# One PSUM ring of four double banks and a new hand-written order, in an attention and maxout-FFN kernel

## The chip, the cores and the metric

The kernel runs on 1 core of one Trainium2 chip. The metric is the device time in microseconds; the time before is the median of 8 runs.

## The reference

Attention over memory slots, then a feed-forward block with a maximum of three products. Batch 8, 8 heads, sequence 576, head size 64, 32 slots, model width 512, d_ff 768; all in float32.

```python
a = np.exp(phi - max_s(phi));  a = a / (sum_s(a) + 1e-09)      # over the sequence
k_m = einsum('bhsm,bhsd->bhmd', a, k);  v_m = einsum('bhsm,bhsd->bhmd', a, v)
attn = softmax_m(q @ k_m.T / 8)                                # over the 32 slots
o = attn @ v_m                                                 # heads side by side: 512 columns
h = max(max(o @ w1, o @ w2), o @ w3)
out = h @ w_out                                                # 4608 x 512
```

## The kernel before

The kernel never forms `o`. As `o @ w` is `attn @ (v_m @ w)`, it folds each batch's 32 slots per head into the weights (8 heads x 32 slots = 256 rows) and multiplies `attn` by the folded weights. It also uses max(x1, x2, x3) = max(x1 - x3, x2 - x3, 0) + x3: w1 - w3 and w2 - w3 are folded, the rectified first difference is compared with the second one, and x3 @ w_out is added through w3 @ w_out, which is worked out once at the start.

Work is cut into steps that are named by a letter, a number and the batch (`F3@2`). Each function issues the instructions of one step, and a text written by hand gives the order of all steps; each engine runs its own instructions in that order. The text lists the steps of the first batches one by one, then a loop runs the same pattern for the middle batches (a `+` after a name is a later batch, a `-` an earlier one), and a last line does batch 7. The steps:

- L0, L1, L2 (lines 92, 99, 107): loads of phi, of k and v, and of q; from batch 1 on all are issued by GpSimd's queue, which also loads the weights at the start and takes its work in order. Each load waits until the buffer of two batches earlier is free.
- E (line 208, ScalarE): exp of phi. B (line 219): 72 small matmuls into `kvp`, the sums over the sequence. N (lines 233 to 243, VectorE): division. K (lines 259, 261): three transposes into `kvtp`, copied by VectorE to `kvt`.
- Q0, Q1 (line 271, VectorE): transposes of q, one per half of the heads. S (lines 293, 302): 32 small matmuls into two `sc` accumulators, and two exps on ScalarE.
- M (line 314): two matmuls for the sums over slots. R (lines 327, 333, ScalarE): logarithm, then exp, for the reciprocal. X (line 338, VectorE): the product, which is `attn`.
- D0 to D3 (line 358): the folds, 8 matmuls each; D0 to D2 make the 1536 columns of `wp` (D0: columns 0 to 511, and so on), D3 makes `wp3`. Each takes a drain of 128 x 1024 out of PSUM (`evacuate`, lines 148 to 158).
- F0 to F11 (lines 383 to 395): first layer, 4 matmuls each into `acc`. An even F is the first difference of a column tile and ends in a relu on ScalarE (`h1`, four buffers), the odd one after it in number ends in a maximum on VectorE that reads `h1`.
- T0 to T4 (lines 411 to 429): second layer, 128 rows of output each, 6 matmuls with w_out and 2 with `wp3` (4 small ones in T4, which spans two batches and comes with odd batches); drained by `evacuate` and stored by SyncE's queue (line 442).
- W, O, V (lines 167, 175, 191): w3 transposed, w3 @ w_out, and the differences of the weights, all only at the start. Z (line 143): dummy matmuls on a tile of zeros.

Accumulators come from two rings of PSUM tiles. `acc_pool` holds three tiles of two banks each, for B, S (two tiles), M, D and F; `one_pool` holds two tiles of one bank, for K, W, O, T and Z. A tile of a ring is taken in the order of the text, and the first matmul into it waits until the tile that was there before has been read.

`EVAC` says who drains: "a" is ScalarE, "v" VectorE, and "s" shares it, half each. The last T is drained by both engines, half each, and stored by two queues.

Of the kernel before, what the change touches and what calls it, by code (L numbers as in the profile page):

```python
# [8 lines left out]
FP32 = mybir.dt.float32  # L9
BF16 = mybir.dt.bfloat16  # L10
# [5 lines left out]
def kernel(  # L16
# [12 lines left out]
    nc = tc.nc  # L29

    B, H, S, D = q.shape
    M = phi.shape[-1]
    P = 128
    NP = H // 2
    NG = NP // 2
# [3 lines left out]
    DM = H * D  # L39
    DF = moe_w1.shape[1]  # L40
    FT = DF // P
# [6 lines left out]
    quad = ctx.enter_context(tc.tile_pool(name="quad", bufs=4))  # L48
    opool = ctx.enter_context(tc.tile_pool(name="opool", bufs=6))
    acc_pool = ctx.enter_context(  # L50
        tc.tile_pool(name="accp", bufs=3, space=bass.MemoryType.PSUM)
    )
    one_pool = ctx.enter_context(
        tc.tile_pool(name="onep", bufs=2, space=bass.MemoryType.PSUM)
    )

    ctx.enter_context(tc.manual_schedule())
# [13 lines left out]
    wo_sb = const.tile([P, FT, DM], BF16, name="wo_sb")  # L71
# [10 lines left out]
    halves = [slice(0, NP // 2), slice(NP // 2, NP)]  # L82
# [55 lines left out]

    def warm_up(n):

        po = one_pool.tile([P, DM], FP32, name="po", tag="one")
        for _ in range(n):
            nc.tensor.matmul(  # L143
                po[:, 0:BANK], lhsT=warm[:, 0:P], rhs=warm, start=True, stop=True
            )


    EVAC = {"D": "asaa", "T": "vaava"}

    def evacuate(kind, n, out_, in_):  # L150
        e = EVAC[kind][n]
        if e == "s":
            nc.scalar.copy(out=out_[:, 0], in_=in_[:, 0])  # L153
            nc.vector.tensor_copy(out=out_[:, 1], in_=in_[:, 1])  # L154
        elif e == "a":
            nc.scalar.copy(out=out_, in_=in_)  # L156
        else:
            nc.vector.tensor_copy(out=out_, in_=in_)  # L158


    def w3_t(f2):

        pt = one_pool.tile([P, 2, NP, P], BF16, name="pt", tag="one")
        for i in range(2):
            f = 2 * f2 + i
            for j in range(NP):
                nc.tensor.transpose(
                    pt[:, i, j, :], w_sb[:, j, 2, f * P : (f + 1) * P], ident
                )
        nc.vector.tensor_copy(out=w3T[:, 2 * f2 : 2 * f2 + 2], in_=pt)  # L170

    def w3_o(j):
        po = one_pool.tile([P, DM], FP32, name="po", tag="one")
        for f in range(FT):
            nc.tensor.matmul(  # L175
                po,
                lhsT=w3T[:, f, j, :],
                rhs=wo_sb[:, f, :],
                start=(f == 0),
                stop=(f == FT - 1),  # L180
            )
        nc.scalar.copy(out=w3o[:, j, :], in_=po)
# [27 lines left out]
    def att_kv(b, js=range(NP)):  # L210
        s = st[b]
        if "kvp" not in s:
            s["kvp"] = acc_pool.tile([P, NG, BANK], FP32, name="kvp", tag="acc")
        kv, kvp = loaded[b]["kv"], s["kvp"]
        for c in range(NC):
            for j in js:
                for a in range(NG):
                    r = slice(HP * a, HP * (a + 1))
                    nc.tensor.matmul(  # L219
                        kvp[M * j : M * (j + 1), a, 0 : 3 * D],  # L220
                        lhsT=s["e"][r, j, c, :],
                        rhs=kv[r, :, j, c, :],
                        start=(c == 0),
                        stop=(c == NC - 1),
                        tile_position=(HP * a, M * j),
                    )
# [26 lines left out]
    def att_kv_t(b):  # L253


        s = st[b]
        ps = one_pool.tile([P, 3, P], BF16, name="kvtp", tag="one")
        for n in range(3):
            nc.tensor.transpose(ps[:, n], s["kvn"][:, n], ident)
        kvt = work.tile([P, 3, P], BF16, name="kvt")  # L260
        nc.vector.tensor_copy(out=kvt, in_=ps)
        s["kvt"] = kvt
# [13 lines left out]
    attns = {}  # L276
# [68 lines left out]
    wps, wp3s = {}, {}  # L345
# [25 lines left out]
    hts = {}  # L371
# [32 lines left out]
    def ffn2(b, t, last=False):  # L404


        hT, attn = hts[b // 2], attns[b // 2]
        po = one_pool.tile([P, DM], FP32, name="po", tag="one")
        c0 = S - HP if t == 4 else (b % 2) * (S + HP) + t * P
        for fc in range(FT):  # L410
            nc.tensor.matmul(  # L411
                po,
                lhsT=hT[:, fc, c0 : c0 + P],
                rhs=wo_sb[:, fc, :],
                start=(fc == 0),
                stop=False,
            )
        for g in range(NG):
            if t < 4:
                nc.tensor.matmul(  # L420
                    po,
                    lhsT=attn[:, g, c0 : c0 + P],
                    rhs=wp3s[b][:, g, :],
                    start=False,
                    stop=(g == NG - 1),
                )
            else:
                for u in range(2):
                    nc.tensor.matmul(  # L429
                        po[HP * u : HP * (u + 1)],  # L430
                        lhsT=attn[:, g, c0 + HP * u : c0 + HP * (u + 1)],
                        rhs=wp3s[b - 1 + u][:, g, :],
                        start=False,
                        stop=(g == NG - 1),
                        tile_position=(0, HP * u),
                    )
        ot = opool.tile([P, DM], FP32, name="ot")
        r0 = (b // 2) * 2 * S + c0
        rows = out[r0 : r0 + P, :]
        if not last:  # L440
            evacuate("T", t, ot, po)
            nc.sync.dma_start(out=rows, in_=ot)
        else:
            h = [slice(0, DM // 2), slice(DM // 2, DM)]
            nc.scalar.copy(out=ot[:, h[0]], in_=po[:, h[0]])
            nc.vector.tensor_copy(out=ot[:, h[1]], in_=po[:, h[1]])
            nc.scalar.dma_start(out=rows[:, h[0]], in_=ot[:, h[0]])
            nc.sync.dma_start(out=rows[:, h[1]], in_=ot[:, h[1]])


    def issue(b, n):

        if not 0 <= b < B or (n == "T4" and b % 2 == 0):
            return
        i = int(n[1:]) if len(n) > 1 else None
        {
            "L": lambda: (load_ph, load_kv, load_q)[i](b),
            "E": lambda: [att_exp(b, h) for h in (halves if b == 0 else [slice(0, NP)])],
            "B": lambda: [att_kv(b, range(NP)[h]) for h in (halves if b == 0 else [slice(0, NP)])],
            "N": lambda: att_kv_norm(b),  # L460
            "K": lambda: att_kv_t(b),
            "Q": lambda: att_q(b, i),
            "S": lambda: att_score(b),
            "M": lambda: att_sum(b, i),
            "R": lambda: att_rec(b, i),
            "X": lambda: att_mul(b, i),
            "D": lambda: fold(b, i),
            "F": lambda: ffn1(b, i),
            "T": lambda: ffn2(b, i),
            "W": lambda: w3_t(i),  # L470
            "O": lambda: w3_o(i),
            "V": lambda: w_diff(i),
            "Z": lambda: warm_up(i),
        }[n[0]]()

    def run(b, text):

        for w in text.split():
            issue(b + w.count("+") - w.count("-"), w.rstrip("+-"))

    for w in """
        E@0 L0@2 Z26@0 B@0 N@0 Z5@0 K@0 Q0@0 Q1@0 L2@2 L1@2 Z18@0 W1@0 W0@0 S@0 M0@0 R0@0
        W2@0 M1@0 O1@0 O0@0 V0@0 R1@0 O3@0 X0@0 X1@0 D0@0 V2@0 O2@0 F6@0 F2@0 F4@0 V1@0 F0@0
        D2@0 D1@0 F7@0 F3@0 E@1 L0@3 F8@0 F1@0 F9@0 F5@0 F10@0 F11@0 B@1 L1@3 D3@0 N@1 K@1
        D0@1 Q1@1 Q0@1 L2@3 D2@1 D1@1 T2@0 S@1 T0@0 E@2 L0@4 M0@1 R0@1 M1@1 X0@1 R1@1 X1@1
        T3@0 T1@0 Q1@2 F0@1 F8@1 F1@1 F9@1 F6@1 F2@1 D3@1 B@2 L1@4 Q0@2 L2@4 F4@1 N@2 F7@1
        K@2 F10@1 F3@1 S@2 F5@1 F11@1 M1@2 E@3 L0@5 M0@2 R1@2 R0@2 T0@1 D0@2 X0@2 D2@2 B@3
        L1@5 N@3 X1@2 T1@1 D1@2 D3@2 Q0@3 Q1@3 L2@5 K@3 E@4 L0@6
    """.split():
        n, b = w.split("@")  # L490
        issue(int(b), n)
    for b in range(2, B - 1):
        run(b, "F6 F0 T4- F7 F4 F1 F2 F10 F3 F8 F5 F9 T2- S+ Q0++ B++ L1++++ D3+ E+++")
        run(b, "L0+++++ N++ T3- M0+ R0+ M1+ F11 X0+ T0 R1+ X1+ Q1++ L2++++ D0+ D2+ D1+")
        run(b, "T1 K++")
    run(B - 1, "T4- F0 F2 F1 F10 F8 F11 F3 T3- F4 F6 F5 F7 F9 T2- T2 T3 T4 T0")
    ffn2(B - 1, 1, last=True)


# [28 lines left out]
```

The softmax here doesn't subtract the row's maximum and nothing guards it: scores larger than these inputs give would overflow.

## Time and profile before

| | us |
|---|---|
| median of 8 runs | 176.22 |
| lowest, highest run | 175.84, 176.6 |
| profiled execution, its own time | 176.6 |
| its span from the first to the last instruction | 174.8 |
| TensorE idle in the span | 16.3 |
| of this before 35 us, and after the last matmul | 8.4, 4.1 |
| dummy matmuls (49) | 12.4 busy |
| DMA engines busy at 90% or more | until about 110 us |

The profile is one execution on the chip. A group's line gives the line of the kernel, engine, operation, tiles, shapes and count; then busy time and the mean duration in ns; then the idle time of the engine just before these instructions and what ended it. A timeline line gives start and duration in microseconds from the start of the span; neighbouring instructions of one kind are merged, with their count. PE is TensorE's matmul, PEld its weight load, DVE VectorE, ACT ScalarE, POOL GpSimd, SP SyncE. The end of a matmul is modelled, so the starts of successive matmuls tell more than its duration.

### The profile page before, as it was taken

Reading aid. Unit: us, or ns where it says so; the run is one execution under the profiler, and the core shown is the slowest. Engines: PE = TensorE matmul, PEld = TensorE weight load, DVE = VectorE, ACT = ScalarE, POOL = GpSimd, SP = SyncE. Lnnn points to the kernel's source line nnn. Section 1 sums busy time; section 2 is a strip of 40 time slices with the busy share of each in tenths; the row PEclk is TensorE's granted clock in tenths of the full one; section 3 lists DMA queues with packets and bytes.
Section 4 is the critical chain, followed back from the end, with each engine's and each line's share of the span. In section 5 each row is a group of like instructions: output and inputs, shape, how many; then the busy total and the mean of one; then the engine's idle time right before and its main releaser. Section 6 shows DMA issues by size and latency. Waiting matters only on the chain.

```text
span 174.8 us, 4442 instructions
## 1 busy us (share of the span) xinstructions
PE 158.5 (91%) x1899; PEld 88.3 (51%) x1921; DVE 103.8 (59%) x160; ACT 108.1 (62%) x162; POOL 28.3 (16%) x43
## 2 busy tenths in 40 slices
PE   7939787697999998999999999999999999999990
PEld 2334443372466454644665456547554565466430
DVE  6408316788389468758774937587748363556110
ACT  4100258937967888579849964898479549952210
POOL 7852111113304131131103010000000000000000
PEclk9999999999999999999999999999999999999999
DMA  6999999999999999999999999522013201311333
GB/s 158 157 204 210 207 210 273 212 247 238 208 327 256 221 268 253 269 248 232 316 245 286 243 241 257 118 94 88 4 64 120 99 23 69 117 60 64 120 120 122
DMA packets 21973, 31.76 MB, mean 182 GB/s; under 512 B 1216, under 2 KB 16576, under 8 KB 21952
## 3 DMA queue, kind: packets, MB, share of 16 engines
q0 software_dynamic: 16080, 21.43, 63.8%
q1 hardware_dynamic: 5728, 9.90, 16.1%
q8 instruction: 15, 0.25, 0.5%
q10 hardware_dynamic: 144, 0.13, 0.2%
q14 instruction: 6, 0.05, 0.1%
HBM read 39.32 MB, written 9.44 MB: 279 GB/s over the span
## 4 chain that ended last, share of the span: by engine, by line
PE 69%; DMA 11%; ACT 8%; DVE 5%; POOL 3%; issue 2%; DVEq 0%; POOLq 0%
PE acc L383 25%; PE po L411 24%; DMA w_sb<-in_moe_w_dram 11%; PE po L420 7%; PE wps L358 4%; PE kvp L219 3%; PE sm L314 2%; ACT wp L156 2%; POOL kvo L99 1%; PE po L429 1%; ACT h L393 1%; PE sc L293 1%; DVE hT L395 1%; ACT wp L153 1%; PE po L175 1%
## 5 line engine op out<-in xcount | busy, mean ns | idle before, releaser
L383 PE MATMUL acc<-attn,wp 128*128 128x288 bf16 x384 | 52.6, 286 | 1.5 <-DVE wp L154 0.9
L411 PE MATMUL po<-wo_sb,hT 128*128 128x512 bf16 x196 | 49.2, 379 | 1.7 <-issue 0.9
L395 DVE TENSOR_TENSOR hT<-acc,h 128x576 bf16<-128x576 f32 x48 | 35.1, 754 | 18.0 <-PE acc L383 12.1
L383 PEld LDWEIGHTS <-wp 128*128 128x128 bf16 x384 | 36.6, 97 | 15.4 <-issue 2.8
L393 ACT ACTIVATE h<-acc 128x576 bf16<-128x576 f32 x48 | 29.4, 652 | 12.5 <-PE acc L383 11.7
L411 PEld LDWEIGHTS <-hT 128*128 128x128 bf16 x216 | 20.0, 98 | 24.2 <-issue 4.3
L156 ACT CAST wp<-wps 128x1024 bf16<-128x1024 f32 x24 | 23.7, 1016 | 3.7 <-PE wps L358 3.7
L156 ACT COPY ot<-po 128x512 f32<-128x512 f32 x19 | 11.3, 596 | 21.2 <-PE po L420 15.7
L158 DVE COPY ot<-po 128x512 f32<-128x512 f32 x16 | 11.1, 691 | 20.2 <-PE po L420 20.2
L271 DVE STREAM_TRANSPOSE qT<-qq 128x1152 bf16<-128x1152 bf16 x16 | 21.6, 1364 | 0.7 <-DMA qq<-in_q_dram 0.7
L302 ACT ACTIVATE e<-sc 128x576 bf16<-128x576 f32 x16 | 9.6, 659 | 16.1 <-PE sc L293 16.1
L420 PE MATMUL po<-wp,attn 128*128 128x512 bf16 x64 | 19.0, 379 | 0.0
L143 PE MATMUL po<-warm 128*128 128x512 bf16 x48 | 12.4, 418 | 1.4 <-DVE warm L131 1.2
L338 DVE TENSOR_TENSOR attn<-e,r 128x576 bf16<-128x576 bf16 x16 | 11.9, 750 | 1.9 <-ACT r L333 1.9
L99 POOL DMA_DIRECT2D kvo<-in_k_dram x9 | 6.7, 747 | 31.4 <-PE kvp L219 23.4
L333 ACT ACTIVATE r<-ln 128x576 f32<-128x576 f32 x16 | 10.9, 683 | 0.5
L219 PE MATMUL kvp<-kvo,e 64*32 64x192 bf16 x576 | 8.4, 243 | 3.1 <-DMA kvo<-in_v_dram 3.1
L327 ACT ACTIVATE ln<-sm 128x576 f32<-128x576 f32 x16 | 10.3, 646 | 1.3 <-PE sm L314 1.3
L208 ACT ACTIVATE e<-ph 128x1152 bf16<-128x1152 f32 (+1 forms) x9 | 9.6, 1070 | 1.7 <-DMA ph<-in_phi_dram 1.7
L420 PEld LDWEIGHTS <-attn 128*128 128x128 bf16 x64 | 6.3, 98 | 7.0
L107 POOL DMA_DIRECT2D qq<-in_q_dram x8 | 6.0, 749 | 22.4 <-DVE qT L271 12.6
L219 PEld LDWEIGHTS <-e 64*32 64x32 bf16 x576 | 7.1, 90 | 4.9 <-issue 4.8
(43 smaller groups left out, 104.5 us busy)
## 6 DMA issues: line engine op xcount, KB each, us to landing
out_dram<-ot SPq DMA_DIRECT2D x35, 256.0 KB, 2.7
qq<-in_q_dram POOLq DMA_DIRECT2D x8, 576.0 KB, 18.3
ph<-in_phi_dram POOLq DMA_DIRECT2D x7, 576.0 KB, 18.0
kvo<-in_k_dram POOLq DMA_DIRECT2D x7, 576.0 KB, 16.3
kvo<-in_v_dram POOLq DMA_DIRECT2D x7, 576.0 KB, 19.1
w_sb<-in_moe_w_dram POOLq DMA_DIRECT2D x3, 768.0 KB, 19.5
wo_sb<-in_moe_w_out_dram POOLq DMA_DIRECT2D x1, 768.0 KB, 17.2
ph<-in_phi_dram SPq DMA_DIRECT2D x2, 288.0 KB, 3.0
```

What stands on the lines that cost most here:

```text
L143: nc.tensor.matmul(po[:, 0:BANK], lhsT=warm[:, 0:P], rhs=warm, start=True, stop=True)
L156: nc.scalar.copy(out=out_, in_=in_)
L158: nc.vector.tensor_copy(out=out_, in_=in_)
L219: nc.tensor.matmul(kvp[M * j : M * (j + 1), a, 0 : 3 * D], lhsT=s["e"][r, j, c, :], rhs=kv[r, :, j, c, :], start=(c == 0), stop=(c == NC - 1),
L271: nc.vector.transpose(out=s["qT"][:, j].rearrange("p j c h r -> p (j c h r)"), in_=loaded[b]["q"][:, j].rearrange("p j c d -> p (j c d)"),)
L333: nc.scalar.activation(out=r, in_=ln, func=AF.Exp, scale=-1.0)
L338: nc.vector.tensor_tensor(out=attns[b // 2][:, g, (b % 2) * S : (b % 2 + 1) * S], in0=s["e2"][:, g, 0:S], in1=s["r", g], op=ALU.mult,)
L383: nc.tensor.matmul(acc[:, h, 0:SH], lhsT=wps[b][:, g, w * DF + ft * P : w * DF + (ft + 1) * P], rhs=attn[:, g, c0 : c0 + SH], start=(g == ...
L393: nc.scalar.activation(out=h1, in_=a, func=AF.Relu)
L395: nc.vector.tensor_tensor(out=hT[:, ft, (b % 2) * S : (b % 2 + 1) * S].rearrange("p (h n) -> p h n", h=2), in0=a, in1=s["h1", ft], op=ALU.max,
L411: nc.tensor.matmul(po, lhsT=hT[:, fc, c0 : c0 + P], rhs=wo_sb[:, fc, :], start=(fc == 0), stop=False,)
L420: nc.tensor.matmul(po, lhsT=attn[:, g, c0 : c0 + P], rhs=wp3s[b][:, g, :], start=False, stop=(g == NG - 1),)
```

## The change

Both PSUM pools become one ring of four tiles of two banks, which all steps share, T, K, W, O and Z too. `EVAC` gives all four folds to ScalarE alone (D1 was shared), and T0 and T4 to ScalarE, T1, T2 and T3 to VectorE. Nine dummy matmuls go between the two halves of batch 0's B, and the other dummies are placed anew: 68 in all instead of 49. The last T (now T0 of batch 7) has a function of its own: two halves of 256 columns, each with its own accumulation, the first drained by VectorE and stored by SyncE's queue while the second is multiplied, the second drained by ScalarE and stored by its queue. The order text is new throughout: the part written out step by step reaches into batch 4, and the loop runs for batches 4 to 6 in place of 2 to 6. Every load, fold and layer step is still issued once. In the new text L2@2 stands ahead of L0@2, L2@3 ahead of L1@3, and L0@6 ahead of L2@5 and L1@5.

```diff
-        tc.tile_pool(name="accp", bufs=3, space=bass.MemoryType.PSUM)
-    )
-    one_pool = ctx.enter_context(
-        tc.tile_pool(name="onep", bufs=2, space=bass.MemoryType.PSUM)
+        tc.tile_pool(name="accp", bufs=4, space=bass.MemoryType.PSUM)
...
-        po = one_pool.tile([P, DM], FP32, name="po", tag="one")
+        po = acc_pool.tile([P, DM], FP32, name="po", tag="acc")
...
-    EVAC = {"D": "asaa", "T": "vaava"}
+    EVAC = {"D": "aaaa", "T": "avvva"}
...
-        if not last:
-            evacuate("T", t, ot, po)
-            nc.sync.dma_start(out=rows, in_=ot)
-        else:
-            h = [slice(0, DM // 2), slice(DM // 2, DM)]
-            nc.scalar.copy(out=ot[:, h[0]], in_=po[:, h[0]])
-            nc.vector.tensor_copy(out=ot[:, h[1]], in_=po[:, h[1]])
-            nc.scalar.dma_start(out=rows[:, h[0]], in_=ot[:, h[0]])
-            nc.sync.dma_start(out=rows[:, h[1]], in_=ot[:, h[1]])
+        evacuate("T", t, ot, po)
+        nc.sync.dma_start(out=rows, in_=ot)
+
+    def ffn2_last(b, c0):
...
+        for i in range(2):
+            c = slice(i * DM // 2, (i + 1) * DM // 2)
+            po = acc_pool.tile([P, DM // 2], FP32, name="po", tag="acc")
+            for fc in range(FT):
+                nc.tensor.matmul(
+                    po,
+                    lhsT=hT[:, fc, c0 : c0 + P],
+                    rhs=wo_sb[:, fc, c],
+                    start=(fc == 0),
+                    stop=False,
+                )
...
+            rows = out[r0 : r0 + P, c]
+            if i == 0:
+                nc.vector.tensor_copy(out=ot[:, c], in_=po)
+                nc.sync.dma_start(out=rows, in_=ot[:, c])
+            else:
+                nc.scalar.copy(out=ot[:, c], in_=po)
+                nc.scalar.dma_start(out=rows, in_=ot[:, c])
+
+    def first_kv():
+        for n, h in enumerate(halves):
+            att_kv(0, range(NP)[h])
+            if n == 0:
+                warm_up(9)
...
     for w in """
-        E@0 L0@2 Z26@0 B@0 N@0 Z5@0 K@0 Q0@0 Q1@0 L2@2 L1@2 Z18@0 W1@0 W0@0 S@0 M0@0 R0@0
-        W2@0 M1@0 O1@0 O0@0 V0@0 R1@0 O3@0 X0@0 X1@0 D0@0 V2@0 O2@0 F6@0 F2@0 F4@0 V1@0 F0@0
-        D2@0 D1@0 F7@0 F3@0 E@1 L0@3 F8@0 F1@0 F9@0 F5@0 F10@0 F11@0 B@1 L1@3 D3@0 N@1 K@1
-        D0@1 Q1@1 Q0@1 L2@3 D2@1 D1@1 T2@0 S@1 T0@0 E@2 L0@4 M0@1 R0@1 M1@1 X0@1 R1@1 X1@1
-        T3@0 T1@0 Q1@2 F0@1 F8@1 F1@1 F9@1 F6@1 F2@1 D3@1 B@2 L1@4 Q0@2 L2@4 F4@1 N@2 F7@1
-        K@2 F10@1 F3@1 S@2 F5@1 F11@1 M1@2 E@3 L0@5 M0@2 R1@2 R0@2 T0@1 D0@2 X0@2 D2@2 B@3
-        L1@5 N@3 X1@2 T1@1 D1@2 D3@2 Q0@3 Q1@3 L2@5 K@3 E@4 L0@6
+        E@0 Z26@0 B@0 N@0 Z5@0 K@0 Q0@0 Q1@0 Z15@0 S@0 Z6@0 M1@0 R1@0 W2@0 W0@0 W1@0 M0@0
+        X1@0 Z4@0 O0@0 O1@0 V0@0 R0@0 X0@0 O2@0 Z3@0 D0@0 V1@0 O3@0 F2@0 F6@0 V2@0 L2@2 F0@0
+        D1@0 F4@0 D2@0 F3@0 E@1 F1@0 F10@0 F7@0 L0@2 F11@0 F8@0 F9@0 F5@0 B@1 N@1 D3@0 K@1
+        D2@1 L1@2 D0@1 Q0@1 Q1@1 T1@0 D1@1 S@1 T3@0 M0@1 L0@3 Q0@2 M1@1 R0@1 R1@1 X0@1 X1@1
+        E@2 T0@0 T2@0 F8@1 Q1@2 F6@1 F7@1 F2@1 L2@3 F3@1 F9@1 F4@1 D3@1 B@2 F10@1 N@2 F5@1
+        F0@1 K@2 E@3 F1@1 F11@1 Q1@3 S@2 T0@1 Q0@3 M0@2 R0@2 X0@2 M1@2 L1@3 L0@4 T4@1 R1@2
+        L2@4 L1@4 T3@1 L0@5 X1@2 D0@2 D2@2 B@3 D1@2 N@3 T2@1 F2@2 K@3 F10@2 F3@2 F0@2 Q0@4
+        S@3 F11@2 F8@2 F4@2 F1@2 M1@3 F9@2 R1@3 E@4 F5@2 Q1@4 M0@3 R0@3 T1@1 F6@2 F7@2 D3@2
+        B@4 X1@3 D2@3 D0@3 T0@2 N@4 L0@6 X0@3 K@4 L2@5 F2@3 D1@3 S@4 T1@2 E@5 F3@3 F8@3 L1@5
+        F9@3 F6@3 F4@3 F10@3 L0@7 M1@4 F5@3 E@6 T2@2 R1@4 M0@4 F0@3 Q1@5 R0@4 F7@3 T3@2 L1@6
+        F1@3 L2@6 F11@3 D3@3 B@5 N@5 D0@4 D1@4 T0@3 X1@4 L1@7 K@5 T1@3 D3@4 Q0@5 D2@4 X0@4
+        L2@7
...
-    for b in range(2, B - 1):
-        run(b, "F6 F0 T4- F7 F4 F1 F2 F10 F3 F8 F5 F9 T2- S+ Q0++ B++ L1++++ D3+ E+++")
-        run(b, "L0+++++ N++ T3- M0+ R0+ M1+ F11 X0+ T0 R1+ X1+ Q1++ L2++++ D0+ D2+ D1+")
-        run(b, "T1 K++")
-    run(B - 1, "T4- F0 F2 F1 F10 F8 F11 F3 T3- F4 F6 F5 F7 F9 T2- T2 T3 T4 T0")
-    ffn2(B - 1, 1, last=True)
+    for b in range(4, B - 1):
+        run(b, "T4- D3+ S+ L2++++ T3- F2 F4 Q1++ F5 F10 F3 F0 F6 F1 F8 M1+ F11 F9")
+        run(b, "L0+++++ F7 R1+ M0+ X1+ T2- R0+ D2+ B++ Q0++ D1+ N++ D0+ L1++++ T1 E+++")
+        run(b, "K++ X0+ T0")
+    run(B - 1, "F2 F10 F6 F3 F11 F0 T2- F1 F4 F8 F9 F7 F5 T3- T4 T4- T3 T2 T1")
+    ffn2(B - 1, 0, last=True)
```

More of the change, by code (lines that the diff above doesn't have):

```diff
@@ L161, in w3_t @@
     def w3_t(f2):
-        pt = one_pool.tile([P, 2, NP, P], BF16, name="pt", tag="one")
+        pt = acc_pool.tile([P, 2, NP, P], BF16, name="pt", tag="acc")
         for i in range(2):
@@ L172, in w3_o @@
     def w3_o(j):
-        po = one_pool.tile([P, DM], FP32, name="po", tag="one")
+        po = acc_pool.tile([P, DM], FP32, name="po", tag="acc")
         for f in range(FT):
@@ L256, in att_kv_t @@
         s = st[b]
-        ps = one_pool.tile([P, 3, P], BF16, name="kvtp", tag="one")
+        ps = acc_pool.tile([P, 3, P], BF16, name="kvtp", tag="acc")
         for n in range(3):
@@ L407, in ffn2 @@
         hT, attn = hts[b // 2], attns[b // 2]
-        po = one_pool.tile([P, DM], FP32, name="po", tag="one")
         c0 = S - HP if t == 4 else (b % 2) * (S + HP) + t * P
+        if last:
+            return ffn2_last(b, c0)
+        po = acc_pool.tile([P, DM], FP32, name="po", tag="acc")
         for fc in range(FT):
@@ L439, in ffn2 @@
         rows = out[r0 : r0 + P, :]
-        if not last:
-            evacuate("T", t, ot, po)
-            nc.sync.dma_start(out=rows, in_=ot)
-        else:
-            h = [slice(0, DM // 2), slice(DM // 2, DM)]
-            nc.scalar.copy(out=ot[:, h[0]], in_=po[:, h[0]])
-            nc.vector.tensor_copy(out=ot[:, h[1]], in_=po[:, h[1]])
-            nc.scalar.dma_start(out=rows[:, h[0]], in_=ot[:, h[0]])
-            nc.sync.dma_start(out=rows[:, h[1]], in_=ot[:, h[1]])
+        evacuate("T", t, ot, po)
+        nc.sync.dma_start(out=rows, in_=ot)
+    def ffn2_last(b, c0):
+        hT, attn = hts[b // 2], attns[b // 2]
+        ot = opool.tile([P, DM], FP32, name="ot")
+        r0 = (b // 2) * 2 * S + c0
+        for i in range(2):
[9 more added lines that the diff above has]
+                )
+            for g in range(NG):
+                nc.tensor.matmul(
+                    po,
+                    lhsT=attn[:, g, c0 : c0 + P],
+                    rhs=wp3s[b][:, g, c],
+                    start=False,
+                    stop=(g == NG - 1),
+                )
+            rows = out[r0 : r0 + P, c]
[10 more added lines that the diff above has]
+                warm_up(9)
     def issue(b, n):
@@ L458, in issue @@
             "E": lambda: [att_exp(b, h) for h in (halves if b == 0 else [slice(0, NP)])],
-            "B": lambda: [att_kv(b, range(NP)[h]) for h in (halves if b == 0 else [slice(0, NP)])],
+            "B": lambda: att_kv(b) if b else first_kv(),
             "N": lambda: att_kv_norm(b),
```

## The prediction

> **What bounds the kernel now.** I read the engine totals first, then the groups, then the timeline, and last the waits.
>
> ```profile
> PE 158.5 (91%) x1899; PEld 88.3 (51%) x1921; DVE 103.8 (59%) x160; ACT 108.1 (62%) x162; POOL 28.3 (16%) x43
> ...
> L383 PE MATMUL acc<-attn,wp 128*128 128x288 bf16 x384 | 52.6, 286 | 1.5 <-DVE wp L154 0.9
> L411 PE MATMUL po<-wo_sb,hT 128*128 128x512 bf16 x196 | 49.2, 379 | 1.7 <-issue 0.9
> ...
> L156 ACT CAST wp<-wps 128x1024 bf16<-128x1024 f32 x24 | 23.7, 1016 | 3.7 <-PE wps L358 3.7
> L156 ACT COPY ot<-po 128x512 f32<-128x512 f32 x19 | 11.3, 596 | 21.2 <-PE po L420 15.7
> L158 DVE COPY ot<-po 128x512 f32<-128x512 f32 x16 | 11.1, 691 | 20.2 <-PE po L420 20.2
> ```
>
> TensorE is the bound, but 91% busy hides stalls, since a matmul's end is modelled (286 ns for 288 columns). So I take the pitch of undisturbed steps from the starts in the timeline (letters as in the order text, X1@0 being step X1 of batch 0): F 0.49 us (4 x 122.5 ns), T 1.725, T4 1.84, a fold D 0.257 (24 matmuls in 0.77), B 0.87, S 0.395, M 0.245, K 0.17, O 1.29, W 0.45. All useful steps add up to 139.7 us. I call **lag** a step's start minus the useful work issued before it; it collects dummies, waits and changes of tile shape. The lag before is 20.8 at the first F (29.5 us), 23.1 at B@1 (38.2), 24.7 at b=1's folds (41.1), 24.6 at its first F (49.6), 26.4 at T0@1 (59.4), 28.0 at b=3's first F (84.1), 28.6 at b=4's (100.4), 30.6 at the end (170.35). From b=3 on it grows by 0.55 a batch, nearly all shape changes; up to 84 us it grows by 7.2 after the first F. That stretch is where an order can win. Two places show why:
>
> ```profile
> 33.31 0.63 ACT L153 CAST wp<-wps 128x512 bf16<-128x512 f32 x1
> 33.98 0.69 DVE L154 CAST wp<-wps 128x512 bf16<-128x512 f32 x1 [1.20 <-ACT wp L153]
> 34.73 3.56 PE L383 MATMUL acc<-attn,wp 128*128 128x288 bf16 x26 [0.30 <-DVE wp L154]
> ...
> 50.46 1.37 DVE L271 STREAM_TRANSPOSE qT<-qq 128x1152 bf16<-128x1152 bf16 x1
> 51.75 1.38 DVE L395 TENSOR_TENSOR hT<-acc,h 128x576 bf16<-128x576 f32 x2
> 52.52 0.34 PEld L383 LDWEIGHTS <-wp 128*128 128x128 bf16 x3 [0.30 <-issue]
> ```
>
> The shared drain isn't parallel: VectorE starts 0.04 us after ScalarE ends, so D1 takes 0.63 + 0.04 + 0.69 = 1.36. Second, a Q transpose stands before F1's max on VectorE; the max ends at 52.50 and the matmul three accumulators later starts at 52.52: the ring of three is the wait (0.49 us).
>
> ```profile
> 170.13 0.59 PE L420 MATMUL po<-wp,attn 128*128 128x512 bf16 x2
> 170.76 0.37 ACT L445 COPY ot<-po 128x256 f32<-128x256 f32 x1 [2.97 <-PE po L420]
> 171.17 0.42 DVE L446 COPY ot<-po 128x256 f32<-128x256 f32 x1 [1.44 <-ACT ot L445]
> 171.62 0.33 SPq L448 DMA_DIRECT2D out_dram<-ot  x1
> ```
>
> At the end too the two halves are drained one after the other.
>
> **The Trainium skill.** "TensorE: Matmul & The Clock Gate", section "Back-to-back issue gap", gives N/2.4 + 2.5 ns warm: 122.5 for 288 columns, and the trace agrees (0.49 per F). The same page, "Why this matters for your kernels", says no idle gap over about 3 us, or the clock drops; the longest gap here is 1.95 us and matmuls behind it keep the 0.215 pitch. "ScalarE: Activation LUTs", "What ACT_TABLE_LOAD costs", says back-to-back instructions overlap by about 93 ns: four relus of 0.652 take 2.28 us here, a pitch of 0.543. "PSUM — Partial Sum Buffer", "Specifications (TRN2)": 8 banks, so four double banks are all there is; no trace line shows banks.
>
> **The change, part by part.** *Engines.* D1 on ScalarE alone: ScalarE +8 x (1.016 - 0.605) = +3.3, VectorE -8 x 0.691 = -5.5. T goes from 19 drains on ScalarE and 16 on VectorE to 11 and 24: -8 x 0.596 = -4.8 and +5.5. Totals near 106.6 and 103.8, no new bound; D1's latency falls from 1.36 to 1.02. No matmul work is added but dummies.
>
> *Dummies.* 68 in place of 49: 19 x 0.215 = 4.1 us. Bounds: 0 to +4.1 (below nothing isn't possible, since the clock is already full). I take 0: the nine stand before v's second half (1.95 us of waiting, 9 x 0.215 = 1.94), fifteen (eighteen before) end at 17.95 as Q1 ends, six cover S's exps until w3 has landed at 19.07, four end at 22.6 before w_out (22.89), three end at 27.4 before the difference V0 (27.9), which waits for w1 landing at 26.6. D0 then starts at 27.94 as now. If these transfers came earlier, each filler would be paid in full.
>
> *How I walk.* Each engine takes its steps in the order of the text. A drain starts 0.20 after its last matmul's pitch ends (F: 29.59 + 0.69, relu at 30.27) and frees its slot 0.02 to 0.06 after it ends (52.50, 52.52). A queue that is backed up moves at the pitch: relu 0.54, fold 0.92, E 1.08, ln and exp of R 0.68 each, max 0.66, Q 1.26, a T drain 0.5 or 0.6. An accumulator waits for the one four before it.
>
> *Start, 29.5 to 41 us.* D0 27.94, O3, F2 29.6, F6, F0. V1's first piece runs at 28.7 and its second when w2 lands (30.35), ends 31.03; D1 31.06, F4 31.4, V2 ends 32.16, D2 32.2. ScalarE, in order with its pitches: O3 30.4, F2, F6, F0 to 32.02, D1 to 32.93, F4 33.5, D2 to 34.39, E@1 to 35.47, F10 to 36.02. So F3 starts 33.05, F1, F10, F7 34.52, F11, F8, F9 36.05, F5, and B@1 could start at 37.03. Its v was issued at 12.70 and landed 24.7 later, at 37.4: B@1 37.4 against 38.3. F3's wait for D1's drain holds F1, F10 and F7 behind it, and through them B@1; v would be the later one anyway. N, K and kvt follow as before, so b=1's first fold is at 40.26, not 41.11: **-0.85**. Its q lands at 40.2, just in time.
>
> *41 to 84 us.* D2, D0, T1 40.95, D1, S 43.0, T3 43.6 (0.1 for T1's drain, behind the Q transposes), M0, M1, T0, T2 to 49.37, so the lag at b=1's F is 24.4 (-0.2 to -0.4: T and folds alternate once more, and T3 waits). Then the ring of four: F7 takes the place of T0 (drained 49.94), F3 that of F8; the Q1@2 transpose ends at 51.5, F7's max at 52.25, F4 starts 52.31 with no wait. D3 52.8, B@2 53.1 (its v landed 51.1), F10 54.0, N, F5, F0, K 55.5, F1, F11, S 56.73, T0@1 at 57.3: lag 24.8 against 26.4, **-1.6** in all so far. Then M0, M1, T4@1 59.65 (its drain stands before R1 on ScalarE, which moves R1, X1 and D0's drain; T3 covers that), T3 61.5, D0, D2, B@3 63.8, D1, T2, F2@2 66.8 (lag 25.1), and F2@3 79.7 (lag 25.85 against 28.0): **-2.2**; of this 0.7 is the old wait for D1's second half before F0@2.
>
> *POOL.* q@2 passes ph@2 (lands near 43; wanted 46). k, v@3 now queue behind q@3, which waits for Q1@1 (42.8): issued 43.7, not 39.6. The transfer queue is full there (v@3 landed 60.1, q@3 63.0), so v@3 lands last, near 63.0, for B@3 at 63.8: cover 0.8 us. L0@6 waits for E@4 (74.5) and holds q@5, k, v@5 behind it, issued 69.2 and 63.1 before; wanted at 89 and 92, and nothing else is queued: cover over 8 us. SP's stores follow T, 35 of them before the last one as now, and halt nothing else.
>
> *84 us to the end.* F2@4 at 102.95, lag 26.9 against 28.7: E@5, E@6 in front of relus and the interleaved T's cost 0.5 more than before here. In the loop the tight points of the ring are: T3 takes T0's place when T4 is absent (T0's drain ends 0.8 after T0, and D3, S, shape change take 0.77), F6 takes that of F5, which stands behind Q1 on VectorE (0.1 to spare). I take stalls of nearly nothing, against 0.2 per batch now (two F's of 0.59), but a shape change more: lag +0.47 a batch. End near 28.8 against 30.6: **-1.8**.
>
> *Tail.* Two halves of 8 matmuls with 256 columns: 16 x 109 ns (an estimate by the formula of the "Back-to-back issue gap") = 1.75, as 8 x 0.215; eight more weight loads of 0.098 lie under matmuls, and if they didn't they would cost up to 0.8. VectorE's half is drained beside the second half's matmuls, so 0.42 + 0.04 go from the path; the last DMA lands 1.8 us after issue on ScalarE's queue, 1.7 on SP's: **-0.4**.
>
> Sum: 174.8 - 1.8 - 0.4 = 172.6 span. Around it lie 1.8 us (profiled execution 176.6), and that execution is 0.4 over the median: 176.22 - 2.2 = **174.0**.
>
> **Rivals.** *Transfers take the win (175.1).* For it: v, q@1 already cap the start (37.4, 40.2), DMA is full to 110 us, and v@3 has 0.8 us of cover. If loads land 1 us later at B@3, 1.1 of the 2.2 goes: -1.1. Against: the queue order only swaps equal sizes.
>
> *The shared ring ties TensorE to ScalarE's queue (177.9, slower).* T0, the folds and E share ScalarE, and each po is now a ring slot. Between F8 and T0's drain ScalarE has 0.54 + 2 x 1.36 + 3 x 0.92 + 1.08 = 7.1 us and TensorE 9.4, so backlog should vanish; but if ScalarE enters it over 2 us late, T0's drain is late, T3 waits in full, and F2 to F8 then meet late slots. The point: over 0.31 us a batch in seven batches eats 2.2. At 0.55 it is 3.9 - 2.2 = +1.7. For it: margins of 0 to 0.1 us; against: the walk finds ScalarE idle before T0 ends.
>
> *No change (176.2).* Fillers or swapped T's give back 2 us of the start. Little speaks for it, since the stalls removed are seen.
>
> **Numbers.** Forecast 174.0, own range 173.1 to 174.9: 0.52. Transfers 175.1: 0.22. No change: 0.06. Ring, or fillers laid bare: 0.20. About 0.2% is what a measurement of this kernel can tell from no change. Faster 0.74, same 0.06, slower 0.20. The range, 172.9 to 176.9, leaves out the worse half of the ring case and a start better than the walk.
>
> **What would show it.** B@1 near 37.4 and b=1's fold near 40.3; T0@1 near 57.3; b=3's first F near 79.7; a chain of waits with no L154; the last copy 0.04 behind the last matmul. It is wrong if kvp waits for in_v at B@3, if acc or po matmuls wait for ot on ScalarE in each batch, or if D0 comes later than 27.9.

## The result and the profile after

The changed kernel takes **173.35 us** (median of 11 runs) against 176.15 for the kernel before in the same sessions: ratio 0.9843, interval 0.9826 to 0.9859, that is 2.8 us less. The profiled execution took 173.35 with a span of 171.6, against 176.6 and 174.8; about 0.4 us of this wider gap is that the profiled execution of before lay above its median.

In the changed file F stands in line 380, the folds in 355, T in 410 and 419, Q in 268, the drains in 153 (ScalarE) and 155 (VectorE). Engine totals and groups of its page:

```profile
PE 161.4 (94%) x1925; PEld 91.7 (53%) x1948; DVE 102.4 (60%) x160; ACT 107.6 (63%) x154; POOL 28.4 (17%) x43
...
L380 PE MATMUL acc<-attn,wp 128*128 128x288 bf16 x384 | 51.2, 286 | 1.1 <-DVE hT L392 0.7
L410 PE MATMUL po<-wo_sb,hT 128*128 128x512 bf16 x191 | 50.1, 379 | 1.1
...
L153 ACT CAST wp<-wps 128x1024 bf16<-128x1024 f32 x32 | 31.3, 1017 | 10.2 <-PE wps L355 10.1
L155 DVE COPY ot<-po 128x512 f32<-128x512 f32 x24 | 16.6, 690 | 30.5 <-PE po L419 30.5
...
L140 PE MATMUL po<-warm 128*128 128x512 bf16 x65 | 18.5, 434 | 1.5 <-DVE warm L128 1.2
...
L153 ACT COPY ot<-po 128x512 f32<-128x512 f32 x11 | 6.4, 586 | 11.4 <-PE po L428 6.3
```

ScalarE and VectorE are as busy as before (107.6 and 102.4 us against 108.1 and 103.8), and TensorE is busy 2.9 us longer in a shorter span; its dummies alone are busy 6.1 us longer (18.5 against 12.4). The gain isn't less work, it is less waiting. Its size can't be read here; the starts of the steps show it. The first place is the first layer of batch 1, where before the ring of three made TensorE wait for a maximum behind a Q transpose. The timeline of the changed kernel there:

```profile
49.72 3.23 PE L380 MATMUL acc<-attn,wp 128*128 128x288 bf16 x25
...
50.16 1.37 DVE L268 STREAM_TRANSPOSE qT<-qq 128x1152 bf16<-128x1152 bf16 x1
51.45 2.17 DVE L392 TENSOR_TENSOR hT<-acc,h 128x576 bf16<-128x576 f32 x3
...
52.88 0.41 PE L355 MATMUL wps<-w3o,kvt 64*32 64x512 bf16 x8
```

The transpose still stands in front of the maxima, but 25 matmuls go through from 49.72 to 52.88 at 0.49 us for four, with no wait. From the first F of batch 1 to T0@1 the lag grows by 0.5, in the kernel before by 1.8. The second place is the tail:

```profile
166.85 0.82 PE L451 MATMUL po<-wo_sb,hT 128*128 128x256 bf16 x6
167.05 0.42 DVE L468 COPY ot<-po 128x256 f32<-128x256 f32 x1 [0.18 <-PE po L459]
...
167.50 0.38 PE L459 MATMUL po<-wp,attn 128*128 128x256 bf16 x2
167.92 0.37 ACT L471 COPY ot<-po 128x256 f32<-128x256 f32 x1 [6.44 <-PE po L459]
168.32 0.37 ACTq L472 DMA_DIRECT2D out_dram<-ot  x1
```

The first half is drained beside the second half's matmuls, and one copy is left behind the last matmul. From the start of the last two matmuls to the end of the span 4.1 us pass (167.50 to 171.6), before 4.7 (170.13 to 174.8). Of this 0.57, 0.2 is that these two are half as wide; 0.4 is the tail's gain.

Two waits are new. The longest of TensorE's waits on the changed kernel, without that at its first instruction (total, times, longest):

```profile
PE kvp L216 <- DMA kvo<-in_v_dram: 1.0, 1, 1.0
PE acc L380 <- DVE hT L392: 0.7, 1, 0.7
PE sm L311 <- DVE hT L392: 0.5, 1, 0.5
```

The wait for v, at B@1, is not new (3.1 us in two places before). The other two are, while the wait for VectorE's half of D1 at F0@2 (0.57 us before) is gone. This is the timeline at the first of them, in the loop's first batch:

```profile
104.19 1.38 DVE L268 STREAM_TRANSPOSE qT<-qq 128x1152 bf16<-128x1152 bf16 x1 [0.84 <-DMA qq<-in_q_dram]
...
105.49 1.38 DVE L392 TENSOR_TENSOR hT<-acc,h 128x576 bf16<-128x576 f32 x2
...
106.26 1.63 PE L380 MATMUL acc<-attn,wp 128*128 128x288 bf16 x12 [0.70 <-DVE hT L392]
```

The wait is put down to VectorE's maximum, but the cause is two steps back: Q1@6 waits 0.84 us for q@6 to land, the maximum of F5 stands behind Q1 in VectorE's queue, and F6 needs the slot that this maximum reads. The same happens at M1@3 with q@4 (0.62 us). The first adds 0.86 to the lag, the second 0.68.

### The profile page after: what moved, and what is told of

It reads as the page before. It is cut to its first block, busy times and chain, and to the rows that moved or that the text cites. A ratio compares the mean times of both kernels' runs of the same rounds, so it can differ in the third digit from the quotient of the medians.

```text
span 171.6 us, 4491 instructions
## 1 busy us (share of the span) xinstructions
PE 161.4 (94%) x1925; PEld 91.7 (53%) x1948; DVE 102.4 (60%) x160; ACT 107.6 (63%) x154; POOL 28.4 (17%) x43
## 4 chain that ended last, share of the span: by engine, by line
PE 43%; DMA 41%; issue 6%; DVE 3%; POOL 3%; ACT 1%; POOLq 0%
DMA kvo<-in_v_dram 20%; PE po L410 16%; PE acc L380 15%; DMA ph<-in_phi_dram 11%; DMA qq<-in_q_dram 10%; PE po L419 5%; POOL kvo L96 3%; PE wps L355 2%; PE kvp L216 2%; DVE qT L268 2%; PE sm L311 1%; PE po L451 1%; PE po L428 1%; ACT e L205 1%; PE sc L290 0%
## 5 line engine op out<-in xcount | busy, mean ns | idle before, releaser
L380 PE MATMUL acc<-attn,wp 128*128 128x288 bf16 x384 | 51.2, 286 | 1.1 <-DVE hT L392 0.7
L410 PE MATMUL po<-wo_sb,hT 128*128 128x512 bf16 x191 | 50.1, 379 | 1.1
L392 DVE TENSOR_TENSOR hT<-acc,h 128x576 bf16<-128x576 f32 x48 | 34.4, 749 | 12.7 <-PE acc L380 8.4
L153 ACT CAST wp<-wps 128x1024 bf16<-128x1024 f32 x32 | 31.3, 1017 | 10.2 <-PE wps L355 10.1
L155 DVE COPY ot<-po 128x512 f32<-128x512 f32 x24 | 16.6, 690 | 30.5 <-PE po L419 30.5
L410 PEld LDWEIGHTS <-hT 128*128 128x128 bf16 x210 | 19.3, 97 | 23.2 <-issue 4.4
L140 PE MATMUL po<-warm 128*128 128x512 bf16 x65 | 18.5, 434 | 1.5 <-DVE warm L128 1.2
L153 ACT COPY ot<-po 128x512 f32<-128x512 f32 x11 | 6.4, 586 | 11.4 <-PE po L428 6.3
L140 PEld LDWEIGHTS <-warm 128*128 128x128 bf16 x68 | 7.0, 109 | 10.6 <-issue 4.4
L89 POOL DMA_DIRECT2D ph<-in_phi_dram x7 | 5.3, 756 | 36.9 <-ACT e L205 33.4
```

The costliest lines, as they stand in the source:

```text
L140: nc.tensor.matmul(po[:, 0:BANK], lhsT=warm[:, 0:P], rhs=warm, start=True, stop=True)
L380: nc.tensor.matmul(acc[:, h, 0:SH], lhsT=wps[b][:, g, w * DF + ft * P : w * DF + (ft + 1) * P], rhs=attn[:, g, c0 : c0 + SH], start=(g == ...
L392: nc.vector.tensor_tensor(out=hT[:, ft, (b % 2) * S : (b % 2 + 1) * S].rearrange("p (h n) -> p h n", h=2), in0=a, in1=s["h1", ft], op=ALU.max,
L410: nc.tensor.matmul(po, lhsT=hT[:, fc, c0 : c0 + P], rhs=wo_sb[:, fc, :], start=(fc == 0), stop=False,)
```

## The experiments

My theory after the result: the order gains by its steps' places, and ring and drains are what it was written for. The rivals were that the ring alone, the drains alone or the tail alone bring the gain. All ratios are to the kernel before, run on the same chip (176.15 to 176.6 us). Where a ratio and the quotient of two medians differ (most in old_T: 1.0178 and 1.023), the ratio is used.

| kernel | us | ratio | interval |
|---|---|---|---|
| changed | 173.35 | 0.9843 | 0.9826 to 0.9859 |
| ring_alone | 176.45 | 1.0001 | 0.9981 to 1.002 |
| drains_alone | 183.34 | 1.0369 | 1.0338 to 1.0399 |
| ring_and_drains | 183.3 | 1.04 | 1.037 to 1.043 |
| whole_d1_in_before | 178.67 | 1.012 | 1.0093 to 1.0147 |
| tail_alone | 176.08 | 0.9961 | 0.9944 to 0.9977 |
| order_on_old_pools | 181.57 | 1.0276 | 1.0242 to 1.0309 |
| old_drains | 181.55 | 1.0267 | 1.0225 to 1.0309 |
| shared_d1 | 174.5 | 0.99 | 0.9859 to 0.994 |
| old_T | 180.43 | 1.0178 | 1.0137 to 1.022 |
| t2_on_scalar | 176.9 | 1.0029 | 1.0011 to 1.0047 |
| no_fillers | 173.82 | 0.9866 | 0.983 to 0.9902 |
| q4_q6_first | 172.51 | 0.9782 | 0.9752 to 0.9813 |

**ring_alone**: the kernel before with one pool.

```diff
-bufs=3 (accp), bufs=2 (onep)
+bufs=4 (accp), for all steps
```

> The order, the drains and the tail of before, only the pools made one ring of four double banks. If the ring itself brings the gain (the F waits of 0.1 to 0.5 us of a ring of three vanish): 174.5 to 175.3, about -1. If the ring only works with an order written for it: 176 to 178, since in the old order each po now takes a slot of the accumulators and the folds wait for the drains of T. I lean to the second, near 176.5.

No change, as I leaned, but the waits are not the ones I named. In the first layer of batch 1 the ring does help: from its first F to T0@1 the lag grows by 1.1 and not 1.8. Another wait takes this back:

```profile
PE acc L380 <- DVE wp L151: 2.0, 6, 0.6
```

L151 is VectorE's half of D1. In the old order F0, the second F of a batch, now takes D1's slot and waits for that serial drain: 0.28 us in each of batches 3 to 6, which is new (the waits in batches 0 and 2 were there before). T0@0 waits for it too, 0.6 us.

**drains_alone**: the kernel before with the new table.

```diff
-    EVAC = {"D": "asaa", "T": "vaava"}
+    EVAC = {"D": "aaaa", "T": "avvva"}
```

> Before, with only the table of drains changed (D1 on ScalarE alone, T as avvva). If the shared drain's latency was a cause (0.37 us less of latency, 0.6 us of waiting before F3@0 and 0.7 before F0@2): 175.0 to 175.7. If ScalarE's queue was the limit at those places: no change, 176.0 to 176.5, or slower.

3.7% slower, far from the first alternative; the second allowed for slower, but gave no size. The timeline of this kernel at 100 us:

```profile
100.23 0.59 ACT L156 COPY ot<-po 128x512 f32<-128x512 f32 x1 [1.10 <-PE po L420]
100.71 0.66 ACT L327 ACTIVATE ln<-sm 128x576 f32<-128x576 f32 x1
101.40 0.69 ACT L333 ACTIVATE r<-ln 128x576 f32<-128x576 f32 x1
101.42 0.41 PE L358 MATMUL wps<-w_sb,kvt 64*32 64x512 bf16 x8 [0.67 <-ACT ln L327]
```

T0's drain is now on ScalarE, and the old order puts it in front of R1. ScalarE stands idle 1.10 us for T0's last matmul while R1's logarithm could run; D1 needs the slot that this logarithm reads and starts 0.05 us after its end, and T1 comes behind D1. The lag at the start of a batch grows by 1.7 each time, not 0.55 (30.1, 31.8, 33.4 and 35.1 at the first F of b=3 to 6).

**ring_and_drains**: both of these in the old order.

> The old order and tail with the ring of four and the new table of drains: the changed kernel without its order. If the order is what makes the parts pay: 178 to 182, since T0's drain stands in front of the second logarithm on ScalarE, as in the run with the drains alone (+1.15 us a batch before T1), less what a fourth slot forgives. If the ring forgives it all: about 176.

As slow as the drains alone, and over the range that I gave: the fourth slot forgives nothing, and the order is what is missing.

**whole_d1_in_before**: `"D": "aaaa"`, nothing else.

> The kernel before with D1 on ScalarE alone and nothing else. The prediction's step: D1's latency falls from 1.36 to 1.02 us, which ends the waits before F3@0 (0.3) and F0@2 (0.7): 175.0 to 175.8. If D1 then queues behind D2 on ScalarE in each batch and holds a slot of the ring of three: 176.5 to 178.

1.2% slower. The wait before F0@2 is shorter, but not gone (0.27 us in place of 0.57, now for ScalarE's drain), and the F's of b=1 lose more: the lag at T0@1 is 27.2 against 26.4. From b=3 on it grows by about 0.9 a batch and not 0.55; 0.2 to 0.3 of the difference comes within the first steps of a batch (the first F's and T4), which stand behind the three folds' drains.

**tail_alone**: only the last T is cut into two halves.

> Before, with only the last T cut into two halves, the first drained and stored beside the second's matmuls. The prediction's own term: -0.4, so 175.75. If the store's landing on ScalarE's queue sets the end and takes longer than SP's: 176.1.

-0.39% (0.23 to 0.56), some 0.7 us (0.4 to 1.0, so the forecast 0.4 is at its edge): of the parts that were run alone, the only one that gains.

**order_on_old_pools**: the changed kernel with three double and two single banks.

> The changed kernel on the old pools (three double and two single banks). If the order brings the gain: 173.5 to 174.5, at most 1 us over the changed kernel's 173.35. If the ring brings it: 175.5 or more, with waits of acc matmuls for VectorE's maximum as in the kernel before. I expect about 175, most of it where two F's stand behind a Q transpose.

2.8% slower. Its first waits on TensorE:

```profile
PE acc L383 <- DVE hT L395: 1.3, 6, 0.3
PE po L413 <- DVE ot L158: 1.2, 2, 0.6
```

Both rings bind, in small pieces: F's wait for a maximum three accumulators back, and T's for the drain of the T or K two before them. The lag grows by 2.1 in b=4 and again in b=5, against 1.05 and 0.2 in the changed kernel.

**old_drains**: the changed kernel with `EVAC` of before. **shared_d1** and **old_T** are its two halves, **t2_on_scalar** is one letter of the second.

```diff
-    EVAC = {"D": "aaaa", "T": "avvva"}
+    EVAC = {"D": "asaa", "T": "vaava"}   # old_drains
+    EVAC = {"D": "asaa", "T": "avvva"}   # shared_d1
+    EVAC = {"D": "aaaa", "T": "vaava"}   # old_T
+    EVAC = {"D": "aaaa", "T": "avava"}   # t2_on_scalar
```

> The changed kernel with the old table of drains (D1 shared, T as vaava). The prediction counted D1's latency (1.36 against 1.02) as a cause at the start only, and the T's as load moved: +0.3 to +1.0, so 173.7 to 174.4. If the order was written for these drains: 175 or more, with waits for L155's or L152's drains in each batch.

> The changed kernel with D1 alone shared again (T stays avvva). In the loop's order VectorE's half of D1 now stands in front of N, and waits for ScalarE's half, which stands behind D2's drain; K waits for N. If that is what made the old drains cost 8 us: +1.2 us in most batches, so 178 to 181. If the T's did it: 173.5 to 174.5.

> The changed kernel with T as vaava again (folds stay aaaa). T2's drain then stands on ScalarE in front of R0 and of D2's drain, and T1 takes D2's slot: in the run with all old drains T1@5 waited 1.2 us for it. If this is the larger part: 177 to 180. If the shared D1 did nearly all of it: 173.5 to 175.

> The changed kernel with T2's drain alone moved to ScalarE (T as avava). In the loop's order T2's drain then stands in front of R0 and of D2's drain on ScalarE, and waits 1.78 us for T2's last matmul while they could run; T1 takes D2's slot. If this one place is the cause of old_T's +7 us: 178.5 to 180.5. If T1's drain on ScalarE (behind the folds, in front of E) is the larger part: 174 to 176.

I was wrong about old_drains (+0.3 to +1.0 expected; some 7.5 us more than the changed kernel). Its halves tell the causes apart: shared_d1 costs 1.0 us, old_T 5.9, so the T's make the difference. The timeline of t2_on_scalar in the loop:

```profile
112.18 0.58 ACT L153 COPY ot<-po 128x512 f32<-128x512 f32 x1 [1.78 <-PE po L419]
...
112.66 0.66 ACT L324 ACTIVATE ln<-sm 128x576 f32<-128x576 f32 x1
...
113.94 2.82 ACT L153 CAST wp<-wps 128x1024 bf16<-128x1024 f32 x3
114.98 1.24 PE L410 MATMUL po<-wo_sb,hT 128*128 128x512 bf16 x5 [1.20 <-ACT wp L153]
```

ScalarE waits 1.78 us for T2's last matmul, with R0 and the three folds' drains behind it. T1 takes D2's slot in the ring and starts when D2's drain ends: 1.20 us late, and the steps behind it with it. That is the mechanism, but this one letter costs 3.3 us (1.0029 against 0.9843), about half of what old_T costs, less than I expected. The other half lies between F2@2 and F2@4, and the timeline of old_T shows it at T0@2:

```profile
79.42 0.59 PE L419 MATMUL po<-wp,attn 128*128 128x512 bf16 x2
80.06 0.69 DVE L155 COPY ot<-po 128x512 f32<-128x512 f32 x1 [1.67 <-PE po L419]
80.66 0.16 DVE L230 RECIPROCAL rden<-kvp 128x2 f32<-128x2 f32 x1
81.21 0.23 PE L256 MATMUL kvtp<-ident,kvn 128*128 128x128 bf16 x1 [1.19 <-DVE kvn L232]
...
84.04 2.74 PE L410 MATMUL po<-wo_sb,hT 128*128 128x512 bf16 x6
```

It is the same thing on the other engine: T0's drain is on VectorE here, in front of N@4. VectorE stands idle 1.67 us for T0's last matmul, and K@4 waits 1.19 for N. The lag at F2@3 is 28.6 against 25.8 in the changed kernel. After these waits the granted clock is 0.50 for 3.4 us (T1's six matmuls take 2.74, and 1.46 at the full clock), which adds another 1.4 to the lag. The trace of old_drains has the two waits, too, without the fall of the clock. The drains of T0 and T1 were not run one by one.

**no_fillers**: 22 of the 68 dummies taken out (Z6, Z4, Z3 and the nine inside the first B).

> The changed kernel without the dummies Z6, Z4, Z3 and the nine in the first B: 46 dummies in place of 68. If they lie in waits for transfers, as predicted: no change, 173.2 to 173.5. If some are paid: up to 4.7 us (22 x 0.215) faster. If they keep the clock full: slower, with a pitch over 0.215 after the gap of 2 us in B@0 or the one before V0.

0.9866 (0.983 to 0.9902): not to be told from the changed kernel. The dummies cost nothing, as predicted, but not because nothing happens without them. The stretches around the gap in B@0, with TensorE's granted clock in the third column from the right:

```profile
10.00:11.00 1.00, 0.14 (x8) 0.00 (x0) 0.00 (x0) 0.00 (x0) 0.27 (x2) 1.00 1.19 200
11.00:12.00 1.00, 0.00 (x0) 0.00 (x0) 0.00 (x0) 0.00 (x0) 0.59 (x1) 1.00 1.20 205
12.00:13.00 1.00, 0.88 (x28) 0.91 (x32) 0.00 (x0) 0.00 (x0) 0.72 (x1) 0.66 1.22 210
13.00:14.00 1.00, 1.00 (x18) 0.42 (x11) 0.31 (x2) 0.00 (x0) 0.02 (x1) 0.50 1.20 209
```

The clock falls to half for 3.4 us and is back at 15.7, long before the first fold (27.9), which waits for w1. With the fillers it stays at 1.00; here that bought nothing that can be measured.

**q4_q6_first**: the changed kernel with two moves among the loads.

```diff
-M1@2 L1@3 L0@4 T4@1 R1@2 L2@4 L1@4
+M1@2 L1@3 T4@1 R1@2 L2@4 L0@4 L1@4
...
-T3@2 L1@6 F1@3 L2@6 F11@3
+T3@2 L2@6 L1@6 F1@3 F11@3
```

> The changed kernel with two moves in the loads' order alone: q@4 ahead of phi@4, and q@6 ahead of k, v@6. The profile of the changed kernel shows VectorE waiting 0.62 us for q@4 and 0.84 for q@6, and TensorE's lag growing by 0.68 and 0.86 just then. If these waits are on the path: 171.8 to 172.5 (-0.9 to -1.5). If the time comes back as another wait, for phi@4 or v@6, or for a drain: 173.0 to 173.5.

172.51 us, 0.9782 (0.9752 to 0.9813): faster than both kernels. The timeline at the place where the changed kernel waited:

```profile
102.46 3.72 PE L380 MATMUL acc<-attn,wp 128*128 128x288 bf16 x29
...
103.27 1.37 DVE L268 STREAM_TRANSPOSE qT<-qq 128x1152 bf16<-128x1152 bf16 x1
...
104.56 1.38 DVE L392 TENSOR_TENSOR hT<-acc,h 128x576 bf16<-128x576 f32 x2
```

Q1@6 starts without a wait, and the F's run through. Both waits on q are gone, and only a small one has come (B@4 waits 0.21 us for v@4): the lag at b=5's first F is 26.4, against 27.3.

## Why the prediction was right

The time lies in the range and near the point (174.0 forecast, 173.35 measured), and the steps can be compared one by one, in the profiled execution. A step's start is here that of its first record on TensorE, weight load or matmul, as for the lags of the kernel before in the prediction; a weight load can lead its matmul by up to 0.2 us, so a growth is sure only to about that.

| step | predicted | measured |
|---|---|---|
| B@1 starts, waiting for v | 37.4 | 37.6 |
| b=1's first fold | 40.26 | 40.45 |
| lag at b=1's first F | 24.4 | 24.2 |
| T0@1 | 57.3 | 57.2 |
| B@3 (its first matmul), v@3's landing | 63.8, 63.0 | 63.6, 63.2 |
| b=3's first F | 79.7 | 79.6 |
| lag at b=4's first F | 26.9 | 26.2 |
| growth of the lag in b=3 | 1.05 | 0.42 |
| growth in b=4 | 0.47 | 1.05 |
| growth in b=5 and b=6 | 0.47 each | 0.20, 0.33 |
| lag at the last T, as at the end | 28.8 | 27.75 |
| tail | -0.4 | -0.4 (alone: -0.7, -0.4 to -1.0) |

**The start and the middle** were right in mechanism and size: the order gains until T0@1, capped by the transfers of v@1, and holds the gain. F4@1, behind the Q transpose, was to start at 52.31 without a wait and starts at 52.30. (One reading is off: in the kernel before, F2@1 waits 0.28 there, from 52.24 to 52.52, and not 0.49.) D0 came at 27.4 rather than 27.9, but that is no gain of the change: it ranged from 27.2 to 28.6 over these traces with the landing of w1, and B@1, which waits for v, evened it out.

**The loop** was mis-sized, and with the wrong sign: from b=3 on the prediction gives 0.4 of the gain back (-2.2 to -1.8), and the trace adds 0.6 (-2.85 at the end). I charged each batch 0.47, one shape change more and next to no stalls; b=5 and b=6 grow by 0.20 and 0.33, against 0.55 before. The forecast end is 1.05 us too late: 0.6 of it lies in b=3, where E@5 and E@6 in front of the relus were charged 0.5 that they did not cost, 0.4 in b=5 and b=6, 0.5 in b=7, and the wait for q@6 in b=4 takes 0.6 back. The ring's tight points held but for that wait: it is at F6, which takes F5's slot behind Q1, where the walk had 0.1 us to spare.

**The loads** are the step that failed. "Nothing else is queued: cover over 8 us" looked at q@5, k and v@5, which stood behind L0@6 and had cover. It missed the loads behind those: q@6 was issued at 86.7, lay 17.5 us in a full transfer queue and landed 0.84 late, and q@4 landed 0.62 late. The transfers did not come in at B@3, where that rival had them, but they took 1.1 us (0.9843 against 0.9782). Without the two waits on q the kernel takes 172.5 (q4_q6_first), which is 1.5 below the point and below my own range of 173.1 to 174.9. That 173.35 lies close to 174.0 is in part luck: what was missed here hides part of what was missed in the loop.

**The dummies** at nothing: held. **Engine totals** were near (forecast 106.6 and 103.8; 107.6 and 102.4 measured), but they are a poor guide: "D1's latency falls" is no gain in the old order (+1.2%), and the T's new owners, which I counted as load moved, are worth 5.9 us to this order (1.0178 against 0.9843). Pricing the edits one by one was the wrong picture; the walk, which took each queue in order and all edits at once, was the right one.

**The slower rival** named a real mechanism, with the wrong place. ScalarE's queue does reach TensorE through the shared ring, but at T1, which takes D2's slot, and when a T's drain stands in front of R and the folds (t2_on_scalar). With T2 on VectorE the changed kernel shows no such wait in the loop, as the prediction's tally said.

## What to carry to other kernels

An order written by hand, the ring that it runs on and the engines that drain it are one design. In the old order the ring gave 0, the drains +3.7 and both +4.0%; the new order without the ring gave +2.8 and without the drains +2.7%; all together gave -1.6%. Not run were the new order with both the old pools and the old drains, and the new kernel with its loads in their old places. Walk the queues for the whole change rather than adding up edits; a drain that is put on an in-order engine costs what stands behind it, while that engine waits for the last matmul (ScalarE 1.78 us at T2, VectorE 1.67 at T0). When a change moves loads, follow every load in the queue to its user, not only those that stand next to the moved one.

## What was not expected of the hardware

A wait of 2.0 us on TensorE (10.1 to 12.1) let the granted clock fall to 0.50 in the run without fillers, while one of 1.95 us at the same place of the kernel before (10.6 to 12.55) left it at 1.00. The length of the wait doesn't settle it. Over the traces with a wait at this place the clock fell after 1.93 (whole_d1_in_before), 1.95 (ring_and_drains) and 1.98 us, each time for 3.4 us, and stayed at 1.00 after 1.94 (drains_alone), 1.95, 2.07 (tail_alone) and 2.27 us (ring_alone). The page "TensorE: Matmul & The Clock Gate" of the Trainium skill, section "Why this matters for your kernels", puts the limit at about 3 us; here a shorter gap was enough, though not each time. What decides it stays open.
